# Windowed attention feeding an RWKV channel mix, fp32 accuracy: GpSimd's elementwise work moved to VectorE and ScalarE, and a planner that counts more

## The chip, the cores and the metric

One core of a Trainium2 chip runs the whole program. The metric is the device time of one execution in microseconds (us). The engines are TensorE (PE in the profile; its weight loads are PEld), VectorE (DVE), ScalarE (ACT), GpSimd (POOL) and SyncE (SP), which only issues the transfers.

## The reference

Attention over a window of 64 positions, for 8 batches of 8 heads, 576 positions and 64 channels a head, and behind it a channel mix in which each position is blended with the one before it:

```
scores = scale * q @ k.T,  kept where 0 <= i - j < 64
attn   = exp(scores - max) / (sum + 1e-9)
x      = (attn @ v), heads side by side            # [8, 576, 512]
xk = mu_k*x + (1-mu_k)*x_prev ; xr = mu_r*x + (1-mu_r)*x_prev
k  = max(xk @ w_k, 0)                              # 512 -> 1024
v  = (k*k) @ w_v                                   # 1024 -> 512
out = v / (1 + exp(-(xr @ w_r)))
```

The three weights reach the kernel as raw 64-bit words, two 32-bit halves each, and are decoded on the chip.

## The kernel before

**Attention.** The 72 blocks of 64 positions go in 36 groups of two. For a group g, TensorE computes the scores (tile `s`, `scores`, L269), VectorE masks, takes the maximum and subtracts it (`pack`, L368), ScalarE takes exp, VectorE sums and inverts (`shares`), GpSimd multiplies by the inverse (`scale`, L395), TensorE transposes the result (tile `t`, `flip`, L398), VectorE masks it into two halves (tile `pt`, `keep`), and TensorE multiplies with the values (tile `x`, `values`, L281). ScalarE copies that into `xu` (`keep_x`). There is one PSUM buffer each for `s`, `t` and `x`, and three for the products below (`m`).

**Channel mix.** It goes in 11 units of 4, 5 and nine times 7 blocks, that is 256, 320 and 448 columns. Every fp32 operand of a product is split into a high part (cast to fp32r) and a low part (the rest), and every product is three matmuls: high by high, high by low, low by high. A unit has 240 matmuls: 96 for `xk @ w_k`, 48 for `xr @ w_r`, 96 for the squares (tile `ks`) by `w_v`. `mix` (L433) makes `xk` and `xr`: VectorE a difference `d` and two blends `e`, ScalarE the high parts, GpSimd the low parts. `k_units` (L538): ScalarE applies Relu, GpSimd squares (tile `kf`), ScalarE casts, VectorE makes the low part. `r_units` (L516): ScalarE takes Tanh and Exp of the product, VectorE clips one and clears the sign of the other (two TENSOR_SCALAR) and joins them (`share`). `v_units` gates and stores.

**Weights.** `load_w` (L174) brings 20 chunks of 512 columns, 512 KB each. `decode` (L188) needs per chunk: ScalarE's Abs, four VectorE operations on tile `wt` (two TENSOR_SCALAR, two SCALAR_TENSOR_TENSOR), ScalarE's cast, and GpSimd's subtraction for the low part.

**The order of the work.** Each step is a `Piece` with an engine, a key and a cost in nanoseconds. `play` (L94) runs the pieces through a trial on these costs: whenever an engine is free, it takes the first piece, in order of its key, whose needs are done and whose buffers are free. The order that comes out is the program order of each engine, which nothing changes later: an instruction that waits holds all behind it on its engine. What the trial believes of a transfer is in `transfer` (L220): 60 ns of SP, and a landing 2.6 us later, or for the first loads (those with no key) a time summed up over `bus`. The loads of groups 2 to 35 have the key of the group two before them (`prefetch`, L418), and all first loads stand ahead of them on SP:

```
594      load("q", 0)
595      load("k", 0)
596      load_w(2)
...
602      load("v", 1)
603      load_w(len(chunks) - len(raw))
```

## Time and profile before

| what | value |
|---|---|
| time, median of 3 runs | 757.5 us (755.1 to 758.32) |
| the profiled execution: time / span | 758.66 us / 757.0 us |
| busy: PE, PEld, DVE, ACT, POOL | 83%, 75%, 64%, 33%, 35% of the span |
| mean granted TensorE clock | 0.941 |
| chain that ended last: PE, DVE, DMA | 48%, 39%, 4% |
| DMA queue q1 | 56.65 MB, 25.2% of 16 engines' span |

The span goes from the first instruction to the last; what the execution's own time has beyond it, 1.66 us, lies outside. All recorded operations go through one helper line (L71 before, L75 in the changed kernel), so they are told apart by tile names: `wt` the weights in decoding, `ws` decoded weights, `s`, `pr`, `t`, `pt`, `x` attention, `xu`, `d`, `e`, `xk`, `xr` the mix, `kf`, `ks` the squares, `th`, `r` the gate, `m` a PSUM bank of products. The fp32 matmuls of attention have two records each.

### The profile page before, as it was taken

What the parts mean: (1) busy time and instruction counts of PE and PEld (TensorE: products, weight loads), DVE (VectorE), ACT (ScalarE), POOL (GpSimd) and SP (SyncE); (2) the same over time, 40 slices, a digit from 0 to 9 for tenths busy, and PEclk for the clock granted to TensorE, in tenths of its full rate; (3) what the DMA queues carried; (4) which work ended last, traced back from release to release, by engine and by line L of the source; (5) the groups of instructions that cost most, each with busy time, mean ns of one, the idle gap of its engine ahead of it and who ended that gap; (6) DMA issues with size and microseconds to landing.
All of it is one profiled execution on the core that took longest, in us unless ns stands there. A gap on an engine that the chain in (4) does not pass through costs nothing.

```text
span 757.0 us, 14856 instructions
## 1 busy us (share of the span) xinstructions
PE 626.3 (83%) x6112; PEld 568.5 (75%) x6112; DVE 481.3 (64%) x854; ACT 252.5 (33%) x498; POOL 264.5 (35%) x257
## 2 busy tenths in 40 slices
PE   0021577799899799989989989999996996998998
PEld 0021576699799689879979879988986995997997
DVE  5059999769658657945855774595595478137141
ACT  2023553453343134314314323423421432142240
POOL 3004654444442332523333243153241425125210
PEclk9995698899999999999999999999998998899999
DMA  8961021332322323141232231123233300000001
GB/s 224 400 167 29 0 57 44 98 90 85 109 76 58 93 69 90 43 129 57 57 103 58 58 93 55 54 67 97 57 85 92 97 2 26 25 1 24 25 1 48
DMA packets 85219, 57.59 MB, mean 76 GB/s; under 512 B 13472, under 2 KB 82592, under 8 KB 85152
## 3 DMA queue, kind: packets, MB, share of 16 engines
q1 hardware_dynamic: 85152, 56.65, 25.2%
q8 instruction: 48, 0.79, 0.4%
q14 instruction: 19, 0.16, 0.1%
HBM read 47.19 MB, written 9.44 MB: 75 GB/s over the span
## 4 chain that ended last, share of the span: by engine, by line
PE 48%; DVE 39%; DMA 4%; ACT 3%; issue 2%; POOL 2%; SPq 1%; POOLq 0%; ACTq 0%; DVEq 0%
PE m L71 42%; DVE e L71 11%; DVE wt L71 8%; DVE d L71 4%; DVE r L71 4%; PE s L71 2%; DVE s L71 2%; DVE pt L71 2%; PE t L71 2%; DVE most L71 2%; DVE sums L71 2%; DVE pr L71 2%; PE x L71 2%; DVE rs L71 2%; POOL pr L71 2%
## 5 line engine op out<-in xcount | busy, mean ns | idle before, releaser
L71 PE MATMUL m<-ks,ws 128*128 128x448 f32 (+2 forms) x1056 | 228.7, 368 | 11.6 <-DVE r L71 5.0
L71 PE MATMUL m<-xk,ws 128*128 128x448 f32 (+2 forms) x1056 | 220.8, 361 | 8.2 <-ACT xk L71 3.6
L71 PEld LDWEIGHTS m<-ks,ws 128*128 128x128 f32 x1056 | 196.4, 198 | 28.5 <-DVE r L71 6.6
L71 PEld LDWEIGHTS m<-xk,ws 128*128 128x128 f32 x1056 | 191.1, 194 | 22.5 <-ACT r L71 3.8
L71 POOL TENSOR_TENSOR kf<-kf 128x448 f32<-128x448 f32 (+2 forms) x88 | 83.2, 948 | 192.2 <-ACT kf L71 192.1
L71 PE MATMUL m<-xr,ws 128*128 128x448 f32 (+2 forms) x528 | 114.6, 363 | 14.3 <-ACT xr L71 10.0
L71 DVE TENSOR_TENSOR ks<-kf,ks 128x448 fp32r<-128x448 f32 (+2 forms) x88 | 56.7, 648 | 91.4 <-ACT ks L71 91.2
L71 PEld LDWEIGHTS m<-xr,ws 128*128 128x128 f32 x528 | 96.3, 195 | 22.4 <-ACT xr L71 10.4
L71 POOL TENSOR_TENSOR xk<-e,xk 128x448 fp32r<-128x448 f32 (+2 forms) x44 | 57.5, 1306 | 117.1 <-ACT xk L71 117.1
L71 PE MATMUL s<-k,q 64*64 64x128 f32 (+1 forms) x1152 | 40.3, 280 | 43.8 <-DMA k<-kT 42.5
L71 ACT CAST ks<-kf 128x448 fp32r<-128x448 f32 (+2 forms) x88 | 47.6, 542 | 85.9 <-POOL kf L71 80.4
L71 ACT ACTIVATE kf<-m 128x448 f32<-128x448 f32 (+2 forms) x88 | 45.6, 518 | 88.3 <-PE m L71 85.5
L71 PEld LDWEIGHTS s<-k,q 64*64 64x64 f32 x1152 | 31.8, 140 | 53.9 <-issue 49.1
L71 DVE TENSOR_TENSOR pt<-t,sides 128x512 f32<-128x512 f32 x72 | 46.2, 683 | 32.8 <-PE t L71 32.8
L71 POOL TENSOR_TENSOR pr<-pr,rs 128x512 f32<-128x512 f32 x36 | 41.5, 1154 | 65.4 <-DVE rs L71 60.1
L71 PE MATMUL t<-ident,pr 128*128 128x128 f32 x144 | 26.3, 313 | 41.2 <-POOL pr L71 41.1
L71 DVE SCALAR_TENSOR_TENSOR r<-m,r 128x448 f32<-128x448 f32 (+2 forms) x44 | 25.5, 581 | 53.7 <-PE m L71 53.7
L71 POOL TENSOR_TENSOR xr<-e,xr 128x448 fp32r<-128x448 f32 (+2 forms) x44 | 54.6, 1241 | 12.6 <-ACT xr L71 12.6
L71 PEld LDWEIGHTS t<-ident,pr 128*128 128x128 f32 x144 | 18.9, 157 | 47.9 <-POOL pr L71 46.4
L71 POOL TENSOR_TENSOR ws<-wt,ws 128x512 fp32r<-128x512 f32 x20 | 27.2, 1361 | 74.4 <-ACT ws L71 65.7
L71 DVE SCALAR_TENSOR_TENSOR e<-d,muk,xu 128x448 f32<-128x448 f32 (+6 forms) x60 | 47.9, 829 | 0.6
L71 DVE COPY_PREDICATED s<-own,s 128x512 f32<-128x512 uint32 (+1 forms) x44 | 24.0, 545 | 36.1 <-PE s L71 35.7
(44 smaller groups left out, 560.8 us busy)
## 6 DMA issues: line engine op xcount, KB each, us to landing
v<-v SPq DMA_DIRECT2D x208, 64.0 KB, 2.6
k<-kT SPq DMA_DIRECT2D x28, 384.0 KB, 4.1
q<-qT SPq DMA_DIRECT2D x32, 256.0 KB, 2.9
w<-w_k SPq DMA_DIRECT2D x8, 512.0 KB, 7.6
w<-w_v SPq DMA_DIRECT2D x8, 512.0 KB, 10.3
outT<-r SPq DMA_DIRECT2D x12, 224.0 KB, 2.0
k<-kT SPq DMA_DIRECT2D x8, 256.0 KB, 3.5
w<-w_r SPq DMA_DIRECT2D x4, 512.0 KB, 5.6
```

Source lines behind the costliest of these rows:

```text
L71: return lambda *args, **kw: tc.keep_in_program_order(op(*args, **kw))
```

## The change

It has four parts.

1. *GpSimd's work goes elsewhere.* The low parts of weights, `xk` and `xr` and the softmax product `scale` go to VectorE (POOL_LOW and POOL_MIX are empty), the squares to ScalarE. GpSimd keeps its constants and the zero columns of `xu`. In the gate, VectorE's two TENSOR_SCALAR go; ScalarE now takes Abs and Relu of the product (which frees the bank) and then Tanh and Exp of these.
2. *Groups 0 to 4 are "lean".* ScalarE takes exp straight from the scores in eight activations of 64 columns, each with its own bias and with the sum as a second result; the subtraction and the sum on VectorE go, a small multiplication by -SCALE comes.
3. *Loads.* The values of a group are loaded once, 2 blocks instead of 3: `values` reads the block before from the tile of group g-1, which is held for longer. The chunks of `w_v` are 256 columns wide, 16 instead of 8, and groups 2 to 5 are loaded between the weights.
4. *The trial counts more.* A transfer costs SP 450 ns an issue and lands by its size over a shared bus; VectorE's operations marked `port` take turns in a `port` clock; TensorE pays for turning from one kind of work to another (TURN); the link between engines costs 160 instead of 80; and from key 60 on TensorE's pieces want their needs done 1500 ns earlier (SLACK). BEGIN's entries for groups 2 to 6 are lower. Decoding, packing and keeping are cut into several pieces.

```diff
-BEGIN = (-30, -28, 2, 14, 24, 34, 43, *range(53, 184, 10),
+BEGIN = (-30, -28, -8, 4, 12, 30, 40, *range(53, 184, 10),
-LINK = 80
+LINK = 160
+RATE = 370
+SLACK = 1500
+STEADY = 60
...
+    def slow(key):
+        return SLACK if key >= STEADY else 0
...
+    TURN = {("m", "s"): 90, ("s", "x"): 30, ("x", "m"): 110, ("m", "x"): 120, ("s", "m"): 110,
+            ("x", "s"): 60, ("x", "t"): 150, ("s", "t"): 150, ("t", "s"): 150, ("t", "x"): 150}
...
-                    if not all(q.done is not None and q.done + (q.lag if q.engine != e else 30) <= now for q in p.needs):
+                    if not all(q.done is not None and q.done + (q.lag + p.slack if q.engine != e else 30) <= now
+                               for q in p.needs):
...
-                    free[e] = now + p.cost
+                    begin = now
+                    if p.port:
+                        begin = max(now, port)
+                        port = begin + p.cost
+                    if e == "PE":
+                        begin += TURN.get((kind, p.kind), 0)
+                        kind = p.last if hasattr(p, "last") else p.kind
+                    free[e] = begin + p.cost
                     p.done = free[e]
+                    if p.size:
+                        bus = max(p.done + 1300, bus) + p.size / RATE
+                        p.lag = bus + 500 - p.done
...
+    chunks = [(ws, w, i, c, wc) for ws, w, wc in ((wr_s, w_r, 512), (wk_s, w_k, 512), (wv_s, w_v, 256))
+              for c in range(w.shape[1] // wc) for i in range(w.shape[0] // P)]
...
-            pool.tensor_sub(ws[i, c][:, 1], words[n], ws[i, c][:, 0].bitcast(F32))
+            LOW[1].tensor_sub(ws[i, c][:, 1], words[n], ws[i, c][:, 0].bitcast(F32))
...
-    def transfer(fn, size, takes=(), needs=(), key=None):
-        p = Piece("SP", len(pieces) - 9999 if key is None else key, 60, fn, needs, takes, lag=2600)
-        if key is None:
-            bus[0] = max(bus[0], 1300) + size / 300
-            p.lag = bus[0] + 900
-        return p
+    def transfer(fn, size, takes=(), needs=(), key=None, count=1):
+        return Piece("SP", len(pieces) - 9999 if key is None else key, 450 * count, fn, needs, takes, size=size)
...
-                for a, (b, i) in enumerate(((b0, i0 - 1), (b0, i0), (b1, i1))):
-                    if i >= 0:
-                        dma.dma_start(x[p * W:(p + 1) * W, :, a], value(b, i, p))
+                    for j in range(2):
+                        if b0 == b1:
+                            dma.dma_start(x[p * W:(p + 1) * W, j], value(b0, i0, p, 2)[:, j])
...
-                                      v[pr, j, s + a, h * W:(h + 1) * W],
+                                      loaded["v", g + (s + a - 1) // 2][pr, j, (s + a - 1) % 2, h * W:(h + 1) * W],
...
+            if gv and block(gv, 0)[1]:
+                uses += [held["v", gv - 1]]
...
+        def exps():
+            s8 = banks[g].rearrange("q h e k -> q (h e) k")
+            for e in range(8):
+                sca.activation(weights[g][:, e], s8[:, e, :W], AF.Exp, scale=SCALE, bias=sums[g][0][:, e:e + 1],
+                               accum_out=sums[g][1][:, e:e + 1])
...
-            pool.tensor_mul(weights[g], weights[g], sums[g][2].unsqueeze(2).to_broadcast([P, 8, W]))
+            dve.tensor_mul(weights[g], weights[g], sums[g][2].unsqueeze(2).to_broadcast([P, 8, W]))
...
-        q = Piece("PE", key + 1, 530, flip, [q], [tbank], [rows], lag=200)
+        q = Piece("PE", key + 1, 430, flip, [q], [tbank], [rows], lag=200, kind="t", slack=slow(key))
...
-                pool.tensor_sub(xs[0][:, 1, c, :n], e[0][:, :n], xs[0][:, 0, c, :n].bitcast(F32))
+                LOW[1].tensor_sub(xs[0][:, 1, c, :n], e[0][:, :n], xs[0][:, 0, c, :n].bitcast(F32))
...
-                sca.activation(state[0], ps[0], AF.Tanh, scale=0.5)
-                sca.activation(state[1], ps[0], AF.Exp)
+                sca.activation(state[0], ps[0], AF.Abs)
+                sca.activation(state[1], ps[0], AF.Relu, scale=-1.0)
+
+            def bounded(state=state):
+                sca.activation(state[0], state[0], AF.Tanh, scale=0.5)
+                sca.activation(state[1], state[1], AF.Exp, scale=-1.0)
...
-                dve.tensor_scalar(r, r, 1.0, None, op0=ALU.min)
-                dve.tensor_scalar(th.bitcast(U32), th.bitcast(U32), 0x7FFFFFFF, None, op0=ALU.bitwise_and)
                 dve.scalar_tensor_tensor(r, th, 1.0, r, op0=ALU.add, op1=ALU.mult)
...
-                pool.tensor_mul(state[0], state[0], state[0])
+                sca.square(state[0], state[0])
...
+    POOL_LOW = set()
+    POOL_MIX = set()
+    LEAN = {0, 1, 2, 3, 4}
+    LOADED = 6
...
-    load_w(len(chunks) - len(raw))
+    load_w(4)
+    bring(2)
+    load_w(4)
+    bring(3)
+    load_w(8)
+    bring(4)
+    load_w(8)
+    bring(5)
```

What this makes of the order shows best at three places. The first is TensorE's program start before; `k_112`, `k_125` and `k_208` are the keys of groups 0, 1 and 2, in that order of their loads.

```order
L71 MATMUL s_179<-k_112,q_108 64x64 x8
L71 MATMUL s_179<-k_112,q_108 64x128 x8
L71 MATMUL s_219<-k_208,q_196 64x128 x16
L71 MATMUL t_262<-ident_82,pr_198 128x128 x4
L71 MATMUL s_274<-k_125,q_123 64x128 x16
L71 MATMUL x_300<-pt_270,v_118 64x64 x24
L71 MATMUL t_370<-ident_82,pr_336 128x128 x4
```

And the same start in the changed kernel, where `k_125` is again group 1 and `k_197` group 2.

```order
L75 MATMUL s_129<-k_112,q_108 64x64 x8
L75 MATMUL s_129<-k_112,q_108 64x128 x8
L75 MATMUL s_206<-k_125,q_123 64x128 x16
L75 MATMUL t_224<-ident_82,pr_150 128x128 x4
L75 MATMUL x_269<-pt_245,v_118 64x64 x24
L75 MATMUL t_322<-ident_82,pr_234 128x128 x4
```

Before, the scores of group 2 stood second; now group 1's do, and group 2's come after the values of groups 0 and 1. The second place is SP's queue, before, from the last loads of `w_v` to the keys of group 2.

```order
L71 DMA w_168<-w_v 128x1024
L71 DMA w_170<-w_v 128x1024
L71 DMA v_172<-v2 64x2x128 x6
L71 DMA q_196<-qT 128x4x128
L71 DMA k_208<-kT 128x4x192
```

In the changed kernel SP's queue around the keys of group 2 reads so:

```order
L75 DMA w512_184<-w_k 128x1024
L75 DMA w512_188<-w_k 128x1024
L75 DMA q_190<-qT 128x4x128
L75 DMA k_197<-kT 128x4x192
L75 DMA v_200<-v2 64x2x128 x4
L75 DMA w512_230<-w_k 128x1024
```

Group 2 was loaded behind all 20 chunks; now it comes behind 8 chunks of 512 columns. The third place is TensorE in the steady part, before, at group 13 (it has a first block of a batch, hence the 64x64): from its scores to its transposition.

```order
L71 MATMUL s<-k,q 64x128 x8
L71 MATMUL s<-k,q 64x64 x8
L71 MATMUL x<-pt,v 64x64 x32
L71 MATMUL m<-ks,ws 128x448 x27
L71 MATMUL t<-ident,pr 128x128 x4
```

The same group in the changed kernel, where weights have the name `w_...`:

```order
L75 MATMUL s<-k,q 64x128 x8
L75 MATMUL s<-k,q 64x64 x8
L75 MATMUL x<-pt,v 64x64 x32
L75 MATMUL m<-ks,w_1260 128x448 x3
L75 MATMUL m<-ks,w_1158 128x448 x3
L75 MATMUL m<-xk,w_443 128x448 x3
L75 MATMUL m<-ks,w_1164 128x448 x3
L75 MATMUL m<-xk,w_490 128x448 x3
L75 MATMUL m<-ks,w_1188 128x448 x3
L75 MATMUL m<-xk,w_543 128x448 x3
L75 MATMUL m<-ks,w_1191 128x448 x3
L75 MATMUL m<-xk,w_615 128x448 x3
```

Fifteen more such matmuls follow before the transposition: it now has 42 product matmuls between it and the values in front of it, where it had 27.

More of the change, by code (lines that the diff above doesn't have):

```diff
@@ L84, in attn_rwkv_kernel, with __init__ @@
     class Piece:
-        def __init__(self, engine, key, cost, fn, needs=(), takes=(), uses=(), lag=LINK, spare=0):
+        def __init__(self, engine, key, cost, fn, needs=(), takes=(), uses=(), lag=LINK, spare=0,
+                     port=False, kind=None, size=0, slack=0):
             self.engine, self.key, self.cost, self.fn = engine, key, cost, fn
@@ L107, in play @@
             now = heapq.heappop(times)
+            while times and times[0] == now:
+                heapq.heappop(times)
             while ends and ends[0][0] <= now:
@@ L130, in play @@
                         heapq.heappush(times, at)
+                    for slack in SLACKS:
+                        heapq.heappush(times, p.done + p.lag + slack)
                     heapq.heappush(ends, (p.done + p.lag, n, p))
@@ new lines, in decode @@
+        LOW = ("POOL", pool) if n in POOL_LOW else ("DVE", dve)
+        p = Piece("ACT", key, 60 + wc, sign, [loaded], takes=[word])
+        p = Piece("DVE", key, 70 + .52 * wc, clamp, [p], port=True)
+        p = Piece("DVE", key, 70 + .52 * wc, shift, [p], port=True)
+        p = Piece("DVE", key, 70 + 1.05 * wc, upper, [p], port=True)
+        p = Piece("DVE", key, 70 + 1.05 * wc, lower, [p], port=True)
+        p0 = Piece("ACT", key, 100 + .83 * wc, first_part, [p])
+        decoded[id(ws), i, c] = p0, Piece(LOW[0], key, (30 + 2.43 * wc) if LOW[0] == "POOL" else 70 + 1.05 * wc,
+                                          second_part, [p0], uses=[word], port=True)
@@ L282, in values @@
         ps = crossed[g] = ps_x.tile([P, 2, 512], F32, name="x")
-        v = loaded["v", g]
         for s in range(2):
@@ L314, in fn @@
                 values(gv)
-        p = Piece("PE", key, cost, fn, needs, takes, uses, lag=200)
+        p = Piece("PE", key, cost - 100, fn, needs, takes, uses, lag=200, kind="x" if gs is None else "s",
+                  slack=slow(key))
+        p.last = "s" if gv is None else "x"
         if gv is not None:
@@ L366, in soften @@
         rows, sm = Hold("pr"), Hold("sums")
+        lean = g in LEAN
+        both = block(g, 0)[1] and block(g, 1)[1]
         def pack():
@@ L437, in mix @@
         pk = None
+        LOW = ("POOL", pool) if u in POOL_MIX else ("DVE", dve)
         if u >= 2:
@@ L486, in mix @@
                 mixing[u] = p
-                p = Piece("DVE", key, over(n), blend, [p], uses=[held["x", u]])
-            p = Piece("ACT", key, acts(n), high, [p])
-            made.append((p, Piece("POOL", key, 40 + 2.45 * n, low, [p], uses=[own_])))
+                p = Piece("DVE", key, over(n), blend, [p], uses=[held["x", u]], port=True)
+            p = Piece("ACT", key, acts(n) + 20, high, [p])
+            made.append((p, Piece(LOW[0], key, over(n) if LOW[0] == "DVE" else 40 + 2.45 * n, low, [p], uses=[own_],
+                                  port=True)))
     mixing = {}
     def weight(w, a, c, m):
-        o = m * P
-        return w[c, o // WC][:, a, o % WC:o % WC + P]
+        o, wc = m * P, WIDTH[id(w)]
+        return w[c, o // wc][:, a, o % wc:o % wc + P]
     opened = [None]
@@ L534, in r_units @@
             p = Piece("ACT", key, 2 * acts(n), powers, [p], [scratch, result], [bank])
-            p = Piece("DVE", key, 210 + 2.09 * n, share, [p], uses=[scratch])
+            p = Piece("ACT", key, 2 * acts(n) + 40, bounded, [p])
+            p = Piece("DVE", key, over(n), share, [p], uses=[scratch], port=True)
             gate.append((state, result, p))
@@ L558, in k_units @@
             p = Piece("ACT", key, acts(n), relu, [p], [scratch], [bank])
-            p = Piece("POOL", key, 40 + 2 * n, square, [p])
-            p0 = Piece("ACT", key, acts(n), high, [p], [result])
-            p1 = Piece("DVE", key, over(n), low, [p0], uses=[scratch])
+            p = Piece("ACT", key, acts(n) + 20, square, [p])
+            p0 = Piece("ACT", key, acts(n) + 20, high, [p], [result])
+            p1 = Piece("DVE", key, over(n), low, [p0], uses=[scratch], port=True)
             k2.append((state, result, (p0, p1)))
@@ L592, in rest, with bring @@
         dve.tensor_scalar(mur1, mur, -1.0, 1.0, op0=ALU.mult, op1=ALU.add)
+    def bring(g):
+        for what in ("q", "k", "v"):
+            load(what, g)
     load("q", 0)
```

131 lines of the change are left out of this document (79 added, 52 removed).

## The prediction

> **What bounds the kernel now.** I first cut the span in three by busy time (the windows view): the first 45 us, the weights' decoding up to 157.27 us, where unit 1's products have begun, and the rest.
>
> ```profile
> 0.00:45.00 45.00, 2.46 (x49) 2.12 (x53) 9.76 (x19) 4.93 (x7) 6.48 (x21) 1.00 0.91 297
> 45.00:157.27 112.27, 66.69 (x853) 60.57 (x846) 100.67 (x161) 51.48 (x111) 55.19 (x52) 0.77 0.19 53
> 157.27:757.00 599.73, 557.11 (x5224) 505.86 (x5218) 370.85 (x675) 196.09 (x380) 202.88 (x184) 0.97 0.22 64
> ```
>
> The columns are length, then busy time of PE, PEld, DVE, ACT and POOL, granted clock, DMA share and GB/s. Three limits follow each other: first nothing computes and the DMA is busy (0.91); then VectorE is busy 100.67 of 112.27 us; then TensorE 557.11 of 599.73. The timeline of all engines says what ends the first stretch, and the waits say what VectorE lost in it.
>
> ```profile
> 38.77 0.39 SPq L71 DMA_DIRECT2D q<-qT  x1
> 40.60 0.38 SPq L71 DMA_DIRECT2D k<-kT  x1
> 44.07 1.61 PEld L71 LDWEIGHTS s<-k,q 64*64 64x64 f32 x32 [38.34 <-issue]
> 44.10 1.98 PE L71 MATMUL s<-k,q 64*64 64x128 f32 x32 [37.97 <-DMA k<-kT]
> ```
>
> ```profile
> DVE s L71 <- PE s L71: 41.9, 7, 29.5
> ```
>
> TensorE stands for 37.97 us on scores whose keys were issued at 40.60, in SP's order behind all of `w_v`. By TensorE's order these are group 2's. Group 1, whose keys went out long before, is queued behind them, and so is the transposition of group 0. VectorE, in its own order, stands 29.5 us for the next scores, with 18 of 20 chunks still to decode. The old trial gave a prefetch 2.6 us to land; here it waited for the whole weight queue.
>
> In the third stretch I read TensorE's longest wait, and then its groups with the idle time ahead of each.
>
> ```profile
> PE t L71 <- POOL pr L71: 33.0, 12, 6.9
> ```
>
> ```profile
> L71 PE MATMUL m<-ks,ws 128*128 128x448 f32 (+1 forms) x960 | 212.9, 373 | 4.5 <-DVE r L71 4.5
> L71 PE MATMUL m<-xk,ws 128*128 128x448 f32 (+1 forms) x906 | 196.1, 366 | 0.0
> L71 PE MATMUL m<-xr,ws 128*128 128x448 f32 (+1 forms) x480 | 104.0, 361 | 0.0
> L71 PE MATMUL x<-pt,v 64*64 64x64 f32 x1830 | 32.3, 218 | 1.5 <-issue 1.1 <-DVE pt L71 0.3
> L71 PE MATMUL s<-k,q 64*64 64x128 f32 (+1 forms) x928 | 31.5, 274 | 0.0
> L71 PE MATMUL t<-ident,pr 128*128 128x128 f32 x120 | 21.3, 305 | 33.0 <-POOL pr L71 33.0
> ```
>
> What this work takes at its best pace comes from TensorE's timeline, from start to start.
>
> ```profile
> 457.10 1.10 PE L71 MATMUL s<-k,q 64*64 64x128 f32 x32
> 458.02 1.11 PE L71 MATMUL x<-pt,v 64*64 64x64 f32 x64
> 459.06 10.58 PE L71 MATMUL m<-xk,ws 128*128 128x448 f32 x51
> 469.48 0.60 PE L71 MATMUL t<-ident,pr 128*128 128x128 f32 x4
> 469.83 5.71 PE L71 MATMUL m<-xk,ws 128*128 128x448 f32 x27
> ```
>
> ```profile
> 705.84 17.15 PE L71 MATMUL m<-xk,ws 128*128 128x448 f32 x84
> 722.83 0.77 PE L71 MATMUL m<-xr,ws 128*128 128x448 f32 x3
> ```
>
> A 448-column matmul: (722.83 - 705.84) / 84 = 0.202 us. Of the 2346 product matmuls, 9 units x 240 = 2160 are such: 437 us. The other 186 have 320 columns, by proportion (an estimate) 0.145 us each: 27 us. 29 sets of scores at 0.92, 29 of values at 1.04 and 30 transpositions at 0.35 us: 67 us. Together 531. The stretch less some 4 us of drain behind the last matmul is 596, so 65 us are lost there: 39 in named waits (33.0 + 4.5 + 1.5), 26 in slower running. Part of these 26 follows the waits:
>
> ```profile
> 695.08 8.50 PE L71 MATMUL m<-ks,ws 128*128 128x448 f32 x33 [2.46 <-DVE r L71]
> ```
>
> Behind this wait of 2.46 us, 33 matmuls take 8.50 us where 33 x 0.202 is 6.7, so a wait costs about 1.7 more. 39 us at some 5 us each (the longest is 6.9) are about eight such waits, 14 us; 12 remain for turning between kinds of work, which the change keeps.
>
> **A rule weighed.** The granted clock is 0.77 in the second stretch, with TensorE idle often, and 0.97 in the third; the 2.46 us wait already had its slow matmuls. The Trainium skill (TensorE: Matmul & The Clock Gate, Part 1) has the clock halve after an idle window of about 3.4 us and return after one as long. By the rule a wait below that would cost only itself, and the 1.7 us would not come back with it; the row says that they do, and I go by the row.
>
> **Part 1, the loads and the trial.** Group 2 is now loaded behind 8 chunks, and TensorE does group 1 first, whose keys need none of that. VectorE can go on where it stood 29.5 us. What is late next is VectorE itself, so its work must be counted up to the same point. Removed or shortened:
>
> ```profile
> L71 DVE SCALAR_TENSOR_TENSOR wt<-w,wt 128x512 uint32<-128x512 uint32 x40 | 38.6, 964 | 1.4
> L71 DVE TENSOR_SCALAR wt<-wt 128x512 f32<-128x512 f32 (+1 forms) x40 | 26.4, 660 | 0.9 <-ACT wt L71 0.2
> ```
>
> ```profile
> 9.20 0.89 DVE L71 TENSOR_SCALAR wt<-wt 128x512 f32<-128x512 f32 x2 [0.19 <-ACT wt L71]
> 10.12 1.42 DVE L71 SCALAR_TENSOR_TENSOR wt<-w,wt 128x512 uint32<-128x512 uint32 x2
> ```
>
> ```profile
> 12.33 1.26 POOL L71 TENSOR_TENSOR ws<-wt,ws 128x512 fp32r<-128x512 f32 x1 [8.73 <-DMA muk<-mu_k]
> ...
> 12.49 2.57 DVE L71 TENSOR_SCALAR wt<-wt 128x512 f32<-128x512 f32 x2
> ```
>
> With GpSimd idle, a chunk's pairs take 0.89 and 1.42 us; with GpSimd inside a subtraction, the same first pair takes 2.57. Without GpSimd's operations, 40 x (0.964 - 0.71) + 40 x (0.66 - 0.445) = 10 + 9 = 19 us go. Added are GpSimd's own pieces; the nearest rows, with VectorE's subtraction for the low part:
>
> ```profile
> L71 DVE TENSOR_TENSOR ks<-kf,ks 128x448 fp32r<-128x448 f32 x72 | 47.8, 663 | 89.1 <-ACT ks L71 89.0
> ...
> L71 DVE TENSOR_TENSOR pr<-s,most 128x512 f32<-128x512 f32 x36 | 24.9, 691 | 1.3
> ...
> L71 ACT ACTIVATE pr<-pr 128x512 f32<-128x512 f32 x36 | 22.7, 630 | 61.2 <-DVE pr L71 61.0
> ...
> L71 DVE TENSOR_SCALAR th<-th 128x448 uint32<-128x448 uint32 x36 | 13.9, 386 | 0.0
> ```
>
> 20 low parts of weights at about 0.65 (13 us), 16 of the short units' mix at about 0.4 (6), six products `scale` at 0.69 (4), and 3 for `w_v` in twice as many pieces: 26 us. The lean groups give back two 0.69 operations each (5 x 1.4 = 7), the gate's clips 3. So 26 - 19 - 7 - 3 = -3: VectorE's work up to there stays as it is. The whole gain would be the 29.5 us. I take off 2, because at the start it must still wait for the first chunks and for group 1's chain, all in its fixed order: **-28 us**. The bounds are -15 (GpSimd's share of the slow rows does not return, and 14 us of the wait come back as smaller ones) and -38 (the 10 us that VectorE idles in the second stretch go too). The eight short activations of a lean group have no row; between one 512-column exp (0.63 us) and eight of them (5.0) I take 2 us, off VectorE's path, since decoding runs beside it.
>
> **Part 2, the steady stretch.** The 33.0 us stand where the softmax chain is late for the transposition. VectorE's blends of the next unit then lie in front of it:
>
> ```profile
> 250.42 1.71 DVE L71 SCALAR_TENSOR_TENSOR e<-d,muk,xu 128x128 f32<-128x128 f32 x2
> 252.05 0.80 DVE L71 SCALAR_TENSOR_TENSOR e<-d,mur,xu 128x128 f32<-128x128 f32 x2
> ```
>
> ```profile
> 280.00:340.00 60.00, 55.92 (x617) 50.40 (x615) 41.07 (x80) 19.78 (x39) 19.84 (x19) 0.97 0.29 83
> ```
>
> The last row is a windows row, for use below. The same blend takes 1.71 us beside GpSimd and 0.80 free of it. Without GpSimd eight of these slots a unit shrink to 0.8, some 5 us a unit. GpSimd's 1.1 us in the chain become 0.69. And the order puts 42 matmuls ahead of group 13's transposition instead of 27, 15 x 0.202 = 3 us of cover. I count on 85% of the waits and of what follows them: 0.85 x (39 + 14) = **-45 us**. Bounds: -53 (all), and -10 (the waits are only moved).
>
> Is there an engine that now stops TensorE? VectorE per unit of about 65 us: 41.07 / 60 x 65 = 44.5 now; eight low parts at 0.66 and four `scale` at 0.69 come (8.0), eight clips at 0.39 go (3.1), contention gives back 5: 44 of a 60 us unit. ScalarE: 19.78 / 60 x 65 = 21.4, and eight squares and eight more gate passes of 448 columns come, by the exp's 0.63 for 512 some 0.55 each (8.8): 30 of 60. In the gate's 48 matmuls (9.7 us) it is nearly full: 16 passes at 0.55 are 8.8, beside an exp of 0.63. But Abs and Relu alone free the bank, and the results are due only with `v`, 96 matmuls later. These cost nothing; if that cover were gone, a fraction of 9 x 2 us.
>
> The values loaded once spare transfers at a DMA share of 0.22, worth nothing. Their price is the longer hold: the load of `v` waits for one more set of values, and behind it on SP stand queries, keys and stores of `r`. Each is issued two groups ahead, so I count 0 (bounds 0 and +5).
>
> **The sum.** Span 757.0 - 28 - 45 = 684. The profiled execution is 1.66 above its span and 1.16 above the runs' median of 757.5: 684 + 1.66 - 1.16 = 684.5. I say 684.
>
> **Rivals.** *The waits are only moved* (15%): transpositions later, but the chain behind them later too, since low parts and `scale` now queue on VectorE itself. Then -28 - 10: 719. For it: the chain passes VectorE five times in a fixed order. Against: 3 us more cover at a place that missed by 5, and 5 us a unit less contention.
>
> *The start gains little* (14%): VectorE's decoding is the limit either way and new waits eat the gap: -15 to -8 with the steady part intact, about 702. The clock rule above would give the same figure another way: only the 39 us come back, 0.85 x 39 = 33, and 757 - 28 - 33 + 0.5 = 696; it is in these 14%, at little weight, since two rows of before contradict it (the 2.46 us wait is one).
>
> *VectorE becomes the pace, and it is slower* (4%): contention gives nothing back and VectorE's waiting in its order stays as large as now, 65 - 44.5 = 20.5 us a unit. Then a unit takes 44.5 + 4.9 + 20.5 = 70 us, 9 x 5 = 45 us more, less 28: about 774. It decides from 28 / 9 = 3 us a unit, that is when VectorE's busy and forced idle time together pass 68 us. Against it: today it idles mostly because TensorE is late, not the other way round.
>
> **How the numbers follow.** The forecast has 65%; 2% are left for no change at all. The forecast's own bounds are 757.5 - 38 - 53 = 666 and, with the weaker ends of both parts (-15 and -35), 707. To reach 8 in 10 the range takes in the first two rivals: 664 to 719. A measurement can tell about 0.5%, 3.8 us, from no change. Faster by more: 0.94; within: 0.02; slower: 0.04.
>
> **What would show it.** Right: TensorE's second set of scores starts before 20 us; VectorE's longest wait in the first 50 us is below 8; unit 1's products are under way at about 128 us instead of 157; `t` waits for `pr` below 8 us in all; the blends are all at 0.8 us a pair; VectorE's busy time stays near 465 to 490. Wrong: a product `m` waiting for `ks` or `xk` from VectorE every unit, or a granted clock that stays low with TensorE dense, since then the 0.202 us do not hold.

## The result, and the profile after

| | before | changed |
|---|---|---|
| median of 4 runs each | 757.38 us (755.1 to 758.32) | 659.56 us (658.1 to 660.74) |
| ratio, 95% interval | | 0.8711 [0.8684, 0.8738] |
| profiled execution: time / span | 758.66 / 757.0 us | 660.74 / 659.0 us |
| busy PE, DVE, ACT, POOL | 83%, 64%, 33%, 35% | 93%, 68%, 53%, 1% |

The kernel became 98 us faster. The forecast of 684 had the direction and the two places right; the time lies 4 us below its range of 664 to 719. Both terms of the sum were too small. One execution of a kernel tried below (a_units6) ran at a granted clock of 0.665 throughout and took 880.02 us where its other execution took 655.74; it is compared with nothing.

The same three stretches in the changed kernel, from the windows view. The columns are those of the prediction's first fence; the third stretch begins where unit 1's products are under way, now at 113.60 us. The fourth row is for use below.

```profile
0.00:45.00 45.00, 20.85 (x248) 16.30 (x248) 34.40 (x80) 26.92 (x86) 2.87 (x19) 1.00 0.92 295
45.00:113.60 68.60, 52.31 (x629) 48.37 (x628) 62.02 (x170) 44.77 (x137) 0.11 (x1) 0.88 0.24 70
113.60:659.00 545.40, 541.78 (x5242) 497.94 (x5236) 348.71 (x697) 279.08 (x542) 0.53 (x5) 1.00 0.22 65
0.00:116.30 116.30, 75.86 (x894) 67.38 (x895) 98.22 (x251) 74.17 (x228) 2.98 (x20) 0.93 0.51 157
```

VectorE was busy 9.76 us of the first 45 before; now it is busy 34.40. TensorE was busy 557.11 of 599.73 us in the steady stretch; now it is 541.78 of 545.40, at a granted clock of 1.00. A window of equal work is needed to compare the starts. Before, 54 of unit 1's matmuls (1 + 41 + 12 on TensorE's timeline) were done at 157.27 us; the same view of the changed kernel shows how many are done at 113.60.

```profile
13.42 1.98 PE L75 MATMUL s<-k,q 64*64 64x128 f32 x32 [7.19 <-ACT pr L75]
...
105.11 1.58 PE L75 MATMUL m<-xk,w 128*128 128x320 f32 x9 [0.17 <-DVE r L75]
106.96 2.46 PE L75 MATMUL m<-xk,w 128*128 128x320 f32 x15 [0.27 <-DVE r L75]
...
109.70 2.00 PE L75 MATMUL m<-xk,w 128*128 128x320 f32 x12
...
113.60 5.11 PE L75 MATMUL m<-xk,w 128*128 128x320 f32 x33
118.55 0.60 PE L75 MATMUL t<-ident,pr 128*128 128x128 f32 x4
```

The first row is the second set of scores, at 13.42 us instead of 44.10. Then 9 + 15 + 12 = 36 of unit 1's matmuls are done at 113.60. The 18 that are missing take 18 x (118.55 - 113.60) / 33 = 2.7 us, so the same work stands at 116.3 us where it stood at 157.27: **the start gained 41 us**. What is left, 599.73 to 545.40 - 2.7 = 542.7, is the steady stretch: **it gained 57 us**. Together that is the 98 of the spans, 757.0 to 659.0.

VectorE's longest wait up to that point shows where most of the 41 came from; the prediction's row of before had 29.5 as the longest of its kind.

```profile
DVE s L75 <- PE s L75: 7.1, 2, 6.4
```

For the whole of it, the windows row of before over its own start:

```profile
0.00:157.27 157.27, 69.15 (x895) 62.69 (x895) 110.43 (x180) 56.41 (x118) 61.66 (x73) 0.84 0.40 123
```

VectorE idled 157.27 - 110.43 = 47 us before and 116.30 - 98.22 = 18 us now: 29 us of the gain. The other 12 are VectorE's own busy time, 110.43 to 98.22, although by the prediction's count 26 us of operations came to it. Its decoding rows in the first 116.3 us:

```profile
L75 DVE SCALAR_TENSOR_TENSOR wt<-w,wt 128x256 uint32<-128x256 uint32 (+1 forms) x56 | 28.7, 532 | 0.0
L75 DVE TENSOR_SCALAR wt<-wt 128x256 f32<-128x256 f32 (+3 forms) x56 | 17.1, 344 | 0.9 <-ACT wt L75 0.8
L75 DVE TENSOR_TENSOR w<-wt,w 128x256 fp32r<-128x256 f32 (+1 forms) x28 | 14.6, 534 | 3.0 <-ACT w L75 3.0
```

The first two were 38.6 and 26.4 us: 19.2 less, as forecast (19). The third is the low parts, 14.6 us where I counted 13 and 3. So the pieces were priced about right, and the total was not; the section on the prediction says why.

In the steady stretch, TensorE's groups with the idle time ahead of each:

```profile
L75 PE MATMUL m<-ks,w 128*128 128x448 f32 (+1 forms) x960 | 201.1, 360 | 0.0
L75 PE MATMUL m<-xk,w 128*128 128x448 f32 (+1 forms) x924 | 197.3, 363 | 0.0
...
L75 PE MATMUL t<-ident,pr 128*128 128x128 f32 x120 | 17.9, 272 | 0.0
```

All idle times are 0.0: the 33.0, 4.5 and 1.5 us of before are gone, not 85% of them. By the prediction's own count (437 + 204 x 0.145 + 67 = 534 us of work) and a drain of 3.6 us behind the last matmul, 545.4 - 534 - 3.6 leaves 8 us lost, where 65 were lost before.

The blends that take 448 columns in one operation, before and in the changed kernel, from the groups kept apart by shape:

```profile
L71 DVE SCALAR_TENSOR_TENSOR e<-d,muk,xu 128x448 f32<-128x448 f32 x12 | 13.4, 1118 | 0.6
L75 DVE SCALAR_TENSOR_TENSOR e<-d,muk,xu 128x448 f32<-128x448 f32 x12 | 8.2, 682 | 0.2
```

The same operation takes 682 ns where it took 1118, now that GpSimd is busy only 0.53 us of the stretch.

### The profile page after: what moved, and what is told of

Its sections match the earlier page's. It is cut to its first block, busy times and chain, and to the rows that moved or that the text cites. A ratio compares the mean times of both kernels' runs of the same rounds, so it can differ in the third digit from the quotient of the medians.

```text
span 659.0 us, 14734 instructions
## 1 busy us (share of the span) xinstructions
PE 614.9 (93%) x6112; PEld 562.6 (85%) x6112; DVE 445.1 (68%) x945; ACT 350.8 (53%) x765; POOL 3.5 (1%) x25
## 4 chain that ended last, share of the span: by engine, by line
PE 87%; DVE 6%; DMA 3%; ACT 2%; issue 1%; SPq 0%; ACTq 0%
PE m L75 74%; PE s L75 5%; PE x L75 5%; PE t L75 3%; DMA w<-w_r 2%; DVE wt L75 2%; DMA w<-w_k 1%; DVE w L75 1%; ACT pr L75 1%; DVE e L75 1%; ACT w L75 0%; DVE most L75 0%; DVE xr L75 0%; DVE s L75 0%; DVE r L75 0%
## 5 line engine op out<-in xcount | busy, mean ns | idle before, releaser
L75 PE MATMUL m<-xk,w 128*128 128x448 f32 (+2 forms) x1056 | 219.8, 359 | 7.1 <-ACT kf L75 6.3
L75 PE MATMUL m<-ks,w 128*128 128x448 f32 (+2 forms) x1056 | 215.1, 356 | 4.0 <-DVE ks L75 2.2
L75 PEld LDWEIGHTS m<-xk,w 128*128 128x128 f32 x1056 | 189.4, 192 | 21.5 <-ACT kf L75 6.9
L75 PEld LDWEIGHTS m<-ks,w 128*128 128x128 f32 x1056 | 188.0, 190 | 17.8 <-DVE ks L75 2.4
L75 PE MATMUL m<-xr,w 128*128 128x448 f32 (+2 forms) x528 | 116.2, 366 | 3.6 <-ACT xr L75 1.8
L75 PEld LDWEIGHTS m<-xr,w 128*128 128x128 f32 x528 | 97.1, 197 | 13.0 <-ACT xr L75 2.9
L75 DVE SCALAR_TENSOR_TENSOR r<-th,r 128x448 f32<-128x448 f32 (+2 forms) x44 | 26.1, 593 | 40.5 <-ACT r L75 40.4
L75 ACT ACTIVATE kf<-kf 128x448 f32<-128x448 f32 (+2 forms) x88 | 48.8, 555 | 2.6
L75 PE MATMUL x<-pt,v 64*64 64x64 f32 x2176 | 41.0, 227 | 3.7 <-ACT w L75 2.1
L75 PEld LDWEIGHTS x<-pt,v 64*64 64x64 f32 x2176 | 39.3, 143 | 5.0 <-ACT w L75 2.4
```

Of the source, the lines that this page charges most:

```text
L75: return lambda *args, **kw: tc.keep_in_program_order(op(*args, **kw))
```

## The experiments

All times are medians in us, each with the kernel before beside it on the same chip at 757.0 to 757.4. Kernels whose names begin with b are the kernel before with one or more parts of the change; those with a are the changed kernel with a part undone.

### The two halves, each alone

**The loads alone** (b_loads). The kernel before gets the new belief on landings and the new order of loads; all operations stay on their engines.

```diff
-        if key is None:
-            bus[0] = max(bus[0], 1300) + size / 300
-            p.lag = bus[0] + 900
+                    if p.size:
+                        bus = max(p.done + 1300, bus) + p.size / RATE
+                        p.lag = bus + 500 - p.done
...
-    load_w(len(chunks) - len(raw))
+    load_w(4)
+    bring(2)
+    load_w(4)
+    bring(3)
...
```

> The kernel before with only the loads changed: groups 2 to 5 between the weights, and the trial counting 450 ns an issue and a shared bus for transfers; GpSimd keeps its work, no slack, no lean groups. Theory A (the start's 41 us are 29 us of VectorE waiting that the load order removes, and 12 us of a faster VectorE, while the steady part is a matter of GpSimd): about 728 us (720 to 735), transpositions still waiting some 33 us behind 120 us. Theory B (VectorE's decoding beside GpSimd is the limit of the start, so that the gap only moves): above 742 us.

Measured: 727.99, ratio 0.9614 [0.9565, 0.9664], 29 us faster. TensorE's second scores, and its longest steady wait (the waits of 160 to 640 us):

```profile
12.81 1.99 PE L72 MATMUL s<-k,q 64*64 64x128 f32 x32 [6.73 <-DMA k<-kT]
```

```profile
PE t L72 <- POOL pr L72: 32.9, 12, 6.9
```

The 37.97 us wait of before is 6.73, and the steady wait stands as it stood (33.0 before). By the count of equal work, 54 of unit 1's matmuls are done at 128.25 us, 29 earlier than before, and what is behind them takes 599.05 us where it took 599.73. So with GpSimd still at work this half is worth what the removed wait of VectorE was worth, 29.5 us, and all of it lies at the start.

**The operations alone** (b_moved). The kernel before keeps its loads and its trial; `scale` and the low parts of `xk` and `xr` go to VectorE, the squares to ScalarE, the gate's clips become ScalarE's passes. The low parts of the weights stay on GpSimd.

```diff
-            pool.tensor_mul(weights[g], weights[g], sums[g][2].unsqueeze(2).to_broadcast([P, 8, W]))
+            dve.tensor_mul(weights[g], weights[g], sums[g][2].unsqueeze(2).to_broadcast([P, 8, W]))
...
-                pool.tensor_mul(state[0], state[0], state[0])
+                sca.square(state[0], state[0])
...
```

> The kernel before with its old loads and old trial, and only GpSimd's work moved (low parts of xk and xr and the softmax product to VectorE, squares and the gate's clips to ScalarE; the low parts of the weights stay on GpSimd, since the trial finds no order otherwise). Theory A (GpSimd beside VectorE makes the softmax chain late; without it the transposition's waits go, slack or no slack): the 38 us wait at the start stays, the steady waits fall from 39 to below 12 us, about 715 us (705 to 725). Theory C (only the trial's slack, which puts more products ahead of a transposition, ends them, and low parts on VectorE lengthen the chain): steady waits of 30 us or more, 740 to 760 us.

Measured: 710.21, ratio 0.9380 [0.9342, 0.9417], 47 us faster. The wait at the start, and the steady one:

```profile
PE s L71 <- DMA k<-kT: 41.6, 2, 36.9
...
PE t L71 <- DVE pr L71: 9.8, 16, 1.8
```

The long wait for the keys at the start is still there, 36.9 us. In the steady stretch the wait for the softmax chain falls from 33 to 9.8 us, in 16 pieces of at most 1.8. The gain of 47 is larger than those 23 us. Some 6 of it lie at the start (54 of unit 1's matmuls are done at 151.7 us), 43 behind it. There the rows show one reason, that the matmuls behind such a short wait run at normal pace:

```profile
540.83 0.63 PE L71 MATMUL t<-ident,pr 128*128 128x128 f32 x4 [1.79 <-DVE pr L71]
541.21 3.89 PE L71 MATMUL m<-ks,ws 128*128 128x448 f32 x18
544.93 0.77 PE L71 MATMUL m<-xk,ws 128*128 128x448 f32 x3
```

From start to start (544.93 - 541.21) / 18 = 0.207 us a matmul.

**Both halves** (b_both) is the two edits together, and the low parts of the weights, which b_moved leaves on GpSimd, go to VectorE too.

> The kernel before with the new loads and with all of GpSimd's work moved (low parts of the weights too), but without slack, turns, port, lean groups, halved chunks or pieces of decoding. Theory A (two separate causes: the load order 29 us, GpSimd's work 47 us, which add): 757 - 29 - 47 = 681 us (676 to 688). Theory D (the parts overlap at the start, where VectorE with the weights' low parts is the limit): 690 us or more.

Measured: 679.62, ratio 0.8983 [0.8941, 0.9025], 77.5 us faster, where 29 + 47 = 76. The halves add up, and the count of equal work shows them apart: 54 of unit 1's matmuls are done at 122.0 us, 35 earlier than before (29 + 6 = 35), and the gain behind them is 43 us, as in b_moved. That leaves about nothing for the weights' low parts. The changed kernel is 20 us faster still, 6 at the start (122.0 to 116.3) and 14 behind it, so something else in the change is worth that much.

### What else is worth 20 us

**The slack** (a_slack0).

```diff
-SLACK = 1500
+SLACK = 0
```

> The changed kernel with SLACK = 0, all else as it is. Theory A: transpositions have little to wait for even without the slack, 660 to 668 us, waits of TensorE behind 120 us below 6 us in all. Theory C: 690 us or more, with 25 us of waits of t for pr back and the slow matmuls behind them.

Measured: 666.57, ratio 0.8803 [0.8768, 0.8839], 7 us slower than the changed kernel. TensorE's waits behind 120 us, of which the changed kernel has none:

```profile
PE t L75 <- DVE pr L75: 3.6, 6, 0.9
```

**Three of the trial's new terms** (a_oldtrial): no slack, no cost for turning, the old link. The belief on transfers, the port and the new costs stay.

```diff
-LINK = 160
+LINK = 80
...
-SLACK = 1500
+SLACK = 0
...
-                        begin += TURN.get((kind, p.kind), 0)
+                        begin += 0
```

> The changed kernel with SLACK = 0, LINK = 80 and no turning costs, so that only the belief on transfers and the engines' costs are new in the trial. Theory A (short chain, cover of little weight): 666 to 671 us, waits of t behind 110 us below 8 us in all. Theory C (the trial's counting carries the steady part): 680 us or more.

Measured: 672.57, ratio 0.8880 [0.8844, 0.8916], 13 us slower than the changed kernel; a little above the 666 to 671 of Theory A, well below Theory C's figure. The link and the turning are worth some 6 us beside the slack's 7.

**Decoding in one piece** (a_onepiece): VectorE's four operations of a chunk follow each other again, as they did before.

```diff
...
-        p = Piece("DVE", key, 70 + .52 * wc, clamp, [p], port=True)
-        p = Piece("DVE", key, 70 + .52 * wc, shift, [p], port=True)
-        p = Piece("DVE", key, 70 + 1.05 * wc, upper, [p], port=True)
-        p = Piece("DVE", key, 70 + 1.05 * wc, lower, [p], port=True)
+        p = Piece("DVE", key, 280 + 3.14 * wc, bits, [p], port=True)
```

> The changed kernel with a chunk's four decoding operations in one piece again, so that they stand back to back on VectorE, each needing the one before. Theory H (part of the start's surplus is that independent operations are put between dependent ones, which lets each begin before the last has drained): VectorE's decoding runs at 2.3 us a 512-column chunk as before instead of four slots of 0.6 and less, the first product of unit 1 moves from 105.1 to 107 to 112 us, 662 to 668 us. Otherwise within 1.5 us of 659.6.

Measured: 664.43, ratio 0.8773 [0.8735, 0.8811], 5 us slower. A chunk on VectorE's timeline:

```profile
37.97 0.88 DVE L75 TENSOR_SCALAR wt<-wt 128x512 f32<-128x512 f32 x2
38.89 1.42 DVE L75 SCALAR_TENSOR_TENSOR wt<-w,wt 128x512 uint32<-128x512 uint32 x2
40.34 0.48 DVE L75 SCALAR_TENSOR_TENSOR e<-xu,muk,e 128x256 f32<-128x256 f32 x1
```

The pair of SCALAR_TENSOR_TENSOR, of which the second needs the first, holds VectorE for 40.34 - 38.89 = 1.45 us, 0.72 each. At equal work, which this kernel reaches at 119.1 us and the changed one at 116.3, VectorE is busy 105.1 us here and 98.2 there. It has done 251 operations in both, and their durations (count times mean of each group) add up to 116.0 and 116.1 us. So the 7 us between them are overlap: in the changed kernel more operations begin before the one ahead is recorded as ended.

**The lean groups** (a_nolean).

```diff
-    LEAN = {0, 1, 2, 3, 4}
+    LEAN = set()
```

> The changed kernel with LEAN empty: groups 0 to 4 subtract and sum on VectorE and take one exp of 512 columns. If VectorE's work at the start sets the end (theory A), its 5 x 1.2 us come back and somewhat more by the fixed order: 664 to 668 us. If ScalarE's eight activations and eight reads of the sum (2.3 us a group) were in the way, the time is the same or shorter: 655 to 661 us.

Measured: 661.65, ratio 0.8745 [0.8715, 0.8775], 2 us slower, between the two expected bands; its interval overlaps the changed kernel's, so it carries little weight.

Of the 20 us these give 7 + 6 + 5 + 2. The halved chunks of `w_v`, the values loaded once and the new BEGIN were not tried singly, so this sum is a sum of single removals and no full account.

### GpSimd's work put back

**The weights' low parts** (a_poollow).

```diff
-    POOL_LOW = set()
+    POOL_LOW = set(range(28))
```

> The changed kernel with the low parts of the weights back on GpSimd (28 subtractions), all else as it is. VectorE loses 14.6 us of work at the start. If GpSimd's operations hold VectorE up by as long as they last less what VectorE saves (theory A: 12 us of the start's gain are GpSimd's silence): 660 to 672 us, the first pairs of a chunk at 1.2 us and more beside them. If the hold is small when other work lies between (theory E): 648 to 657 us, and a better kernel.

Measured: 670.16, ratio 0.8858 [0.8824, 0.8891], 10.6 us slower than the changed kernel. GpSimd's group and VectorE's decoding groups:

```profile
L75 POOL TENSOR_TENSOR w<-wt,w 128x256 fp32r<-128x256 f32 (+1 forms) x28 | 34.9, 1257 | 72.3 <-ACT w L75 70.0 <-DMA w<-w_v 2.0 <-DVE e L75 0.4
...
L75 DVE SCALAR_TENSOR_TENSOR wt<-w,wt 128x256 uint32<-128x256 uint32 (+1 forms) x56 | 31.7, 588 | 0.0
...
L75 DVE TENSOR_SCALAR wt<-wt 128x256 f32<-128x256 f32 (+3 forms) x56 | 24.1, 463 | 0.5 <-ACT wt L75 0.5
```

Taking 28 operations (14.6 us) off VectorE makes the start slower: 3.0 + 7.0 = 10 of the 14.6 us come back as longer decoding operations beside GpSimd, and a low part takes GpSimd 1.26 us where it took VectorE 0.53. The rest comes back in its other operations. At equal work (125.3 us here) VectorE's durations add up to 116.3 us, as many as with the low parts; it is busy 3 us longer than in the changed kernel and idle 6 us longer, more of it behind ScalarE. In the order of b_both the same move was worth about nothing, so its price depends on the order around it.

**The mix's low parts** (a_poolmix).

```diff
-    POOL_MIX = set()
+    POOL_MIX = set(range(11))
```

> The changed kernel with the low parts of xk and xr back on GpSimd (POOL_MIX = all units; the trial counts its port and reorders), all else as it is. Theory A (VectorE and GpSimd hold each other up): the blends are slow again (above 1.2 us a pair instead of 0.8) and TensorE waits 8 to 25 us behind 120 us: 668 to 690 us. Theory C (the slack covers a late chain): within 1% of 659.6 us though the blends are slow.

Measured: 661.21, ratio 0.8733 [0.8693, 0.8772], the same as the changed kernel. Theory A's 668 to 690 missed. The blend is slow again, by shape:

```profile
L75 DVE SCALAR_TENSOR_TENSOR e<-d,muk,xu 128x448 f32<-128x448 f32 x12 | 12.2, 1018 | 1.1 <-DVE d L75 0.5
```

It is 1018 ns where it was 682, and yet TensorE waits for nothing behind 113 us. So in the new order, with the slack, GpSimd's interference with the blends, whose end I made a reason of the steady gain, costs nothing. Whether it was part of the loss in the order of before, no run shows by itself.

### Which of order and engine removes the steady wait

**The slack without the move** (b_slack): b_loads, with the slack of 1500 ns on TensorE's pieces from key 60 on. GpSimd keeps all its work.

```diff
+SLACK = 1500
+STEADY = 60
...
-                    if not all(q.done is not None and q.done + (q.lag if q.engine != e else 30) <= now for q in p.needs):
+                    if not all(q.done is not None and q.done + (q.lag + p.slack if q.engine != e else 30) <= now for q in p.needs):
...
```

> The kernel before with the new loads and SLACK = 1500 from key 60 in the trial, GpSimd keeping all its work. Theory C (cover is enough: the transposition only has to come later): steady waits of t for pr fall from 33 to below 8 us, about 685 us (675 to 697). Theory A (GpSimd's hold on VectorE is the cause; 1.5 us of cover cannot hide waits of 5 to 7): 15 to 25 us of waits stay, 705 to 722 us.

Measured: 704.02, ratio 0.9305 [0.9271, 0.9340], 24 us faster than b_loads, just below Theory A's 705 to 722. TensorE's waits behind 120 us:

```profile
PE m L74 <- DVE r L74: 7.6, 3, 3.2
PE x L74 <- issue: 5.6, 3, 2.2
PE t L74 <- POOL pr L74: 5.0, 1, 5.0
```

The slack alone takes the 33 us of waits for the softmax to 5.0, as Theory C had it, and some other waits come in their place. Moving the operations took them to 9.8 with no slack. On top of b_loads the move is worth 48 us (6 of them at the start) and the slack 24; in the changed kernel, with the move, the slack is worth 7. They cover the same loss and don't add up.

### What a wait costs behind it

The prediction charged each wait 1.7 us of slow matmuls. b_loads has the very wait that this came from, 28 us earlier:

```profile
666.94 6.94 PE L72 MATMUL m<-ks,ws 128*128 128x448 f32 x33 [2.46 <-DVE r L72]
673.72 0.77 PE L72 MATMUL m<-xk,ws 128*128 128x448 f32 x3
```

After 2.46 us, 33 matmuls take 673.72 - 666.94 = 6.78 us, 0.205 each: normal. In the kernel before they took 8.50 us after the same 2.46. b_slack has such a wait too, of 2.47 us, with the same normal pace behind it. So the row I went by did not carry the rule I made of it. In the kernel before itself the rule happened to hold: slow matmuls follow each of its eight steady waits of 2.3 to 6.9 us, 1.5 to 3.0 us lost by start-to-start times, some 15 in all. To see more lengths, **a_delay** makes the softmax chain of 13 groups longer with 5 to 14 useless copies on ScalarE (one execution).

```diff
+    DELAY = {9: 5, 11: 6, 13: 7, 15: 8, 17: 9, 19: 10, 21: 11, 23: 12, 25: 13, 27: 14, 29: 6, 31: 8, 33: 10}
...
+            for _ in range(DELAY.get(g, 0)):
+                sca.copy(weights[g], weights[g])
```

> The changed kernel with a softmax chain that is made longer at 13 groups from 9 to 33: behind exp, ScalarE copies the weights onto themselves 5 to 14 times, which the trial does not know (the result stays). TensorE's order stays as it is, so that it has to wait at single transpositions for 0 to some 7 us with dense work around. By the step of the prediction each wait of 2 us and more costs about 1.7 us more behind it. By the Trainium skill (TensorE: Matmul & The Clock Gate, Part 1) the clock halves after an idle window of about 3.4 us, counted by a free-running window: waits below some 2 us never followed by slow matmuls, those between in part of the cases, those above 3.5 always, with about 1.7 us lost each. Time: 690 to 730 us.

Measured: 742.91 against 757.37 for the kernel before, above the expected 690 to 730: behind 110 us TensorE waits 57 us in all. Waits of several lengths on TensorE's timeline, with what follows each:

```profile
187.41 0.98 PE L75 MATMUL m<-ks,w 128*128 128x448 f32 x3 [1.84 <-ACT r L75]
188.19 1.05 PE L75 MATMUL t<-ident,pr 128*128 128x128 f32 x4
...
253.81 1.09 PE L75 MATMUL t<-ident,pr 128*128 128x128 f32 x4 [3.50 <-DVE pr L75]
254.54 4.83 PE L75 MATMUL m<-xr,w 128*128 128x448 f32 x12
...
504.23 1.09 PE L75 MATMUL t<-ident,pr 128*128 128x128 f32 x4 [8.43 <-DVE pr L75]
504.97 6.89 PE L75 MATMUL m<-xk,w 128*128 128x448 f32 x24
...
536.88 0.63 PE L75 MATMUL t<-ident,pr 128*128 128x128 f32 x4 [2.27 <-DVE pr L75]
537.26 3.89 PE L75 MATMUL m<-xr,w 128*128 128x448 f32 x18
541.09 1.10 PE L75 MATMUL s<-k,q 64*64 64x128 f32 x32
```

After 3.50 us, 12 matmuls take 4.83 instead of 2.4; after 8.43, 24 take 6.89 instead of 4.8: some 2 us lost each time, no more for the longer wait. Over all nine of its waits of 3.5 us and more the loss is 1.3 to 3.1 us, with no growth by length. After 2.27 us, 18 take 541.09 - 537.26 = 3.83, 0.213 each, near normal. The 1.84 us wait shows the slow kind all the same (3 matmuls in 0.98 where 0.77 is usual, the next transposition 1.05 where 0.63 is). In a_delay's nine waits of 3.5 us and more and in b_slack's one, slow matmuls follow every time. In the kernel before, b_loads, b_moved, b_slack and a_delay, those from 1.7 to 3.2 whose releaser the view names are mixed: 1.76, 1.84, 2.31, 3.07 and 3.10 slow, 1.77, 1.79, 1.91, 2.27, 2.47 and 3.18 not, and 2.46 both ways. The windows view has the granted clock right behind the waits of 3.50 and 2.27 us, the third figure from the end:

```profile
253.81:257.30 3.49, 3.49 (x11) 3.19 (x12) 2.25 (x4) 1.56 (x4) 0.00 (x0) 0.50 0.00 0
537.26:541.00 3.74, 3.74 (x21) 3.28 (x19) 2.43 (x5) 2.69 (x7) 0.00 (x0) 1.00 0.02 4
```

So the slow matmuls are those under a halved granted clock.

The Trainium skill (TensorE: Matmul & The Clock Gate, Part 1) has the clock halve after at least one idle window of about 3.4 us, and lets these windows run on their own. The rows from 3.5 us on agree with this better than with my 1.7 us for each wait: slow matmuls follow every time, and the loss of about 2 us doesn't grow with the length. The slow matmuls behind 1.76 to 3.10 us, shorter than such a window, don't follow from it, and the expectation's bounds of 2 and 3.5 us are not in it. What decides between two equal waits was not tried.

### Was it SP's queue or the order?

**The old order of loads under the new trial** (a_oldload): all of `w_v` is issued ahead of group 2's loads again, and the trial knows when these land.

```diff
-    LOADED = 6
+    LOADED = 2
...
-    load_w(4)
-    bring(2)
-    load_w(4)
-    bring(3)
-    load_w(8)
-    bring(4)
-    load_w(8)
-    bring(5)
+    load_w(len(chunks) - len(raw))
```

> The changed kernel with the loads in the old order (all weights ahead of group 2), but with the new trial, which knows that group 2 lands late and so leaves group 1 second on TensorE. Theory F (the order that TensorE and VectorE got from a wrong belief made the 29.5 us wait, not SP's queue by itself): VectorE's longest wait in the first 50 us stays below 8 us, 660 to 668 us. Theory G (the queue itself is the cost, since groups 2 and 3 come late for unit 1 in any order): 672 us or more.

Measured: 657.54, ratio 0.8682 [0.8656, 0.8707], no slower than the changed kernel, 2 us faster. SP's timeline, and VectorE's longest wait in the first 116 us:

```profile
20.08 16.16 SPq L75 DMA_DIRECT2D w<-w_v  x16
36.64 0.38 SPq L75 DMA_DIRECT2D q<-qT  x1
37.23 0.38 SPq L75 DMA_DIRECT2D k<-kT  x1
```

```profile
DVE s L75 <- PE s L75: 7.0, 2, 6.3
```

Group 2's keys go out at 37.23 us, nearly as late as the 40.60 of before, and VectorE's longest wait is 6.3 us and not 29.5. So the long wait came from an order built on a landing that did not happen, and the place in SP's queue costs nothing once the order allows for it. Under the new trial, the loading of groups between the weights was no part of the gain.

### A better version

With the products in the steady stretch free of waits, the start is what is left. **a_units6_again** makes the units 5 times 6 and 6 times 7 blocks instead of 4, 5 and 9 times 7.

```diff
-UNITS = (4, 5) + (7,) * 9
+UNITS = (6,) * 5 + (7,) * 6
...
-BEGIN = (-30, -28, -8, 4, 12, 30, 40, *range(53, 184, 10),
+BEGIN = (-30, -28, -26, -8, 2, 12, 20, 34, 48, 63, 76, 90, 103, *range(113, 184, 10),
...
-        if 1 <= t <= 2:
+        if 1 <= t <= 3:
```

> The kernel with units of 6 and 7 blocks again, because its profiled execution was at a clock of 0.665 throughout and one other at 655.7 us was not. If the longer first unit pays: 648 to 657 us. If the low clock comes with this kernel: most executions far above 700 us.

Measured: 655.3, ratio 0.8654 [0.8620, 0.8687], 4 us below the changed kernel. The same kernel had been run before as a_units6 (655.74 us), expected at 645 to 656 us if the longer first unit paid. **a_units6_oldload** puts the old order of loads on top, as in a_oldload, with three groups loaded first.

> The same units, with all weights but the first eight chunks loaded in one go behind group 2, and the other groups behind them, since the old load order was no worse in the changed kernel. If the order that the trial makes matters and SP's queue does not: within 3 us of the run with units of 6 and 7 blocks, 645 to 657 us. If groups 3 and 4 come too late for unit 1: 660 us and more.

Measured: 652.12, ratio 0.8609 [0.8584, 0.8635], 7 us below the changed kernel, and the best of all. Against a_units6_again it is 3.2 us, hardly more than the 3 us within which no difference was expected, and the intervals overlap. TensorE has no wait in the steady stretch here either, so the gain lies at the start and in the sizes of the units; which of the two was not tried.

## Why the prediction was right, and where it fell short

**What bound the kernel** was read rightly: VectorE at the start, behind a wait for scores, and TensorE behind it, with 65 us lost. b_loads and b_moved take the two apart, and b_both has their sum.

**The start, -28 forecast, -41 measured.** The part from VectorE's idle time was right: 29 us, and 29 us in b_loads, which has only that. The step that failed is "26 - 19 - 7 - 3 = -3: VectorE's work up to there stays as it is". It measured -12. The decoding got shorter by what I counted (19 forecast, 19.2 measured); with only GpSimd's weight subtractions put back, 10 of it return (a_poollow). Even the sum of durations came out near the forecast: over equal work the counts times means of all of VectorE's groups add up to 116.9 us before and 116.1 in the changed kernel. What I took wrongly was to price an operation by the duration of its record (0.65 to 0.69 us) and to add durations up. VectorE's busy time, in which overlapping records count once, is 110.43 and 98.22 us: 6 us of overlap before, 18 now. VectorE's timeline of the changed kernel, between 15 and 18 us, shows how:

```profile
15.49 0.68 DVE L75 SCALAR_TENSOR_TENSOR wt<-w,wt 128x512 uint32<-128x512 uint32 x1
16.09 0.69 DVE L75 COPY_PREDICATED s<-own,s 128x512 f32<-128x512 uint32 x1
16.69 0.68 DVE L75 TENSOR_TENSOR pt<-t,sides 128x512 f32<-128x512 f32 x1
17.29 0.68 DVE L75 TENSOR_REDUCE most<-s 128x8 f32<-128x512 f32 x1
18.01 0.17 DVE L75 TENSOR_SCALAR most<-most 128x8 f32<-128x8 f32 x1
```

Independent neighbours start 0.60 us apart although each lasts 0.68; the last pair, of which the second needs the first's result, starts 0.72 apart. The added operations stand between others, and the decoding that stood in dependent pairs is now cut into pieces with other work in between. a_onepiece undoes only this cutting: 7 of the 12 us of busy time come back and the kernel is 5 us slower. What in the new order makes the other 5 us of overlap, no run isolates.

The loads' new order was not needed for this: a_oldload takes it back in the changed kernel at no cost, so there the trial's belief does it. The prediction named both, the queue and the order, and did not tell them apart.

**The steady stretch, -45 forecast, -57 measured.** The mechanism, a late softmax chain, was right. Two sizes failed. "I count on 85% of the waits and of what follows them": all 39 us of waits went. And "12 remain for turning between kinds of work, which the change keeps": only 8 us are lost in all, so at most 8 remain. 39 of waits and 18 of the 26 us of slow running make the 57. Of the reasons none is shown alone. b_moved has 43 of the 57 us with no slack, by a shorter chain and the end of contention at once; b_slack has 24 by cover alone; a_poolmix brings the contention back at no cost, but under the new order, and a_slack0 takes only the slack and costs 7 us.

**The rule weighed.** I went by one row, a wait of 2.46 us with 1.7 us of slow running. For the kernel before the sum held, 14 us forecast and some 15 read there. As a rule it fails: b_loads, b_slack and a_delay show that a wait below 3.2 us may or may not be followed by it. The figure of 1.7 us was near (about 2 us where it happens); "each wait" was wrong. Since all waits went, the choice hardly moved the result. But the clock rule's 696 was not borne out either: it supposed that only the named waits come back, and 18 us more did.

**Counted at nothing.** ScalarE's new passes cost nothing visible: no steady wait for ScalarE appears. The longer hold of the values shows no wait either. The lean groups I put at 2 us of ScalarE's time; they are worth about 2 us.

**The rivals.** Waits only moved (719): no, none are left in the steady stretch. The start gains little (702): no. VectorE as the pace (774): no; it is busy 348.71 of 545.40 us.

**The signs.** Second scores before 20 us: 13.42. VectorE's longest wait at the start below 8: 6.4. `t` for `pr` below 8 us: none in the steady stretch, though 9.1 us in three waits at the start, which the sign did not except. Blends at about 0.8 a pair: the pairs take 0.76 to 0.81. Missed in the good direction: unit 1's products at 105 to 116 us, not 128, and VectorE busy 445 us, not 465 to 490.

The range was too narrow below because its lower end, 757.5 - 38 - 53, took every wait back and still held VectorE's busy time and the turning at their value of before.

## What to carry to other kernels

- Where a planner's order is fixed at build time, look first for a wait that the planner did not believe in; correct the belief before moving transfers. Here belief and new load order together gave 29 us (b_loads), and in the changed kernel the old load order was no slower (a_oldload); the belief alone on the kernel before was not tried.
- Price an operation added to VectorE by start-to-start time among independent neighbours, and work in dependent chains by start-to-start within the chain: here 0.60 and 0.72 us for the same 0.68 us record. Interleaving chains is worth something by itself (5 us in a_onepiece).
- Two cures for one late chain (a faster chain, more work ahead of it) don't add up; try each alone before crediting either.

## What was not expected of the hardware

- VectorE accepts an independent operation 0.08 us before the one ahead of it is recorded as ended (0.60 against 0.68 at 128x512 fp32), and a dependent one some 0.04 after.
- Work for VectorE can be cheaper on VectorE than off it: with 28 low parts (14.6 us) on GpSimd, VectorE's other operations become longer by as much, 112 of decoding by 10 us, and the kernel takes 10.6 us more (a_poollow). It depends on the order: b_both moved them for about nothing.
- Behind waits of 3.5 us or more matmuls run at a granted clock of 0.50 for a loss of 1.3 to 3.1 us that doesn't grow with the wait; behind 1.7 to 3.2 us it happens in some cases only (the same wait of 2.46 us slow in the kernel before, not in b_loads).
